# A threshold shift in rows of three in and rows of two out, half of each pair of batch 1 turned on TensorE, and no early projection of batch 0

## The chip, the cores and the metric

One core of one Trainium2 chip runs the whole program. The metric is device time in microseconds (us) of that core; below 2% counts as "same". Engines as the profile names them: PE (TensorE matmuls), PEld (its weight loads), DVE (VectorE), ACT (ScalarE), POOL (GpSimd), SP (SyncE, which issues most DMAs).

## The reference

```python
scores = q @ k.T / sqrt(64)                          # 8 batches, 8 heads, 576 x 64 each
thresh = max(scores, axis=-1) - tau                  # tau = 0.02
attn   = softmax(where(scores >= thresh, scores, -1e9))
x      = (attn @ v) as rows of 4608 x 512
h      = x @ w_in                                    # 512 x 2048
out    = (h - tanh(h)) @ w_out                       # 2048 x 512
```

## The kernel before

Two heads form a pair, four pairs a batch. A pair has nine tiles of 128 query rows: one mixed tile (rest rows of both heads) and four duos (two tiles, A and B). Tile by tile, in one static order: PE makes the scores, DVE evicts them and takes the row maximum, DVE turns the maximum into `tau - max` (the shift), ACT applies a very steep Prelu (the kink), the result is transposed on PE or by DMA, ACT takes exp, PE multiplies by V. The feed-forward layers of batch m run between the tiles of batch m+1: 16 hidden steps and 16 quarter projections, each four 128x512 matmuls. POOL prepares q, k and v.

The parts that the change touches:

```python
def on_pe(i):                          # which tiles are transposed on PE
    p, j = divmod(i, TPP)              # p: pair, j: tile of the pair
    return p < 6                       # all of batch 0, pairs 4 and 5 of batch 1
...
mx = const.tile([P, 3], F32)           # maxima of a duo; the third column stays 0
...
def shift(i):                          # once per duo, once per mixed tile
    n = 3 if kd == "B" else 1
    nc.vector.tensor_scalar(out=nb[:, 0:n], in0=mx[:, 0:n],
                            scalar1=-1.0, scalar2=tau, op0=ALU.mult, op1=ALU.add)
...
def split(p, t):                       # POOL, meanwhile, for each of q and k
    nc.gpsimd.tensor_scalar(out=x, in0=x, scalar1=QKSC, ...)          # 0.67 us
    nc.gpsimd.tensor_copy(out=hl[:, :, 0, :], in_=x)                  # 0.66 us
    nc.gpsimd.tensor_tensor(out=hl[:, :, 1, :], in0=x, in1=..., op=ALU.subtract)  # 1.28 us
...
pl, tag = (ps_h, "h") if i % 2 and i < HPAIR * TPP else (ps_y, "y")  # PSUM for PE's transposes
...
EARLY = lambda m: 3 if m else 3        # quarter projections done inside their own batch
```

## Time and profile before

| | us |
|---|---|
| timed runs, median (lowest to highest) | 549.77 (549.69 to 550.95) |
| the profiled run | 543.29 (span of the core 541.5) |
| duo shifts (128), in the profile | 41.0, mean 0.320 each |

### The profile page before, as it was taken

What the parts mean: (1) busy time and instruction counts of PE and PEld (TensorE: products, weight loads), DVE (VectorE), ACT (ScalarE), POOL (GpSimd) and SP (SyncE); (2) the same over time, 40 slices, a digit from 0 to 9 for tenths busy, and PEclk for the clock granted to TensorE, in tenths of its full rate; (3) what the DMA queues carried; (4) which work ended last, traced back from release to release, by engine and by line L of the source; (5) the groups of instructions that cost most, each with busy time, mean ns of one, the idle gap of its engine ahead of it and who ended that gap; (6) DMA issues with size and microseconds to landing.
All of it is one profiled execution on the core that took longest, in us unless ns stands there. A gap on an engine that the chain in (4) does not pass through costs nothing.

```text
span 541.5 us, 12959 instructions
## 1 busy us (share of the span) xinstructions
PE 506.7 (94%) x4704; PEld 288.0 (53%) x4771; DVE 445.9 (82%) x1203; ACT 438.3 (81%) x628; POOL 291.1 (54%) x390
## 2 busy tenths in 40 slices
PE   5999898989999999999999999999999999999997
PEld 3666565555555555555555555555555455444444
DVE  4999988989988999889888998899888887554440
ACT  4999888999898989899888989898989989533330
POOL 7999996767555666666545654566665620000000
PEclk9999999999999999999999999999999999999999
DMA  7554657999898998889999899698969975301113
GB/s 207 174 183 146 205 179 141 184 186 170 196 186 151 185 188 189 161 179 184 185 185 183 182 187 197 154 181 185 188 165 182 197 148 105 101 20 40 39 41 78
DMA packets 204768, 85.76 MB, mean 158 GB/s; under 512 B 172320, under 2 KB 197152, under 8 KB 204704
## 3 DMA queue, kind: packets, MB, share of 16 engines
q1 hardware_dynamic: 204112, 84.51, 72.6%
q8 instruction: 37, 0.61, 0.5%
q10 hardware_dynamic: 592, 0.43, 0.3%
q14 instruction: 27, 0.22, 0.1%
HBM read 36.70 MB, written 9.44 MB: 85 GB/s over the span
## 4 chain that ended last, share of the span: by engine, by line
PE 62%; DVE 24%; issue 5%; ACT 5%; DMA 3%; SPq 0%; DVEq 0%; ACTq 0%; POOL 0%
PE psY L510 18%; PE psH L484 16%; PE psS L319 13%; DVE sc L329 12%; PE psO L429 4%; DVE g L503 4%; PE psS L309 3%; PE ps_k L233 2%; PE psHt L484 2%; ACT pT L392 2%; ACT z L363 2%; DVE yo L520 2%; DMA qT<-qhl 2%; DVE nb L343 2%; DVE kT L256 1%
## 5 line engine op out<-in xcount | busy, mean ns | idle before, releaser
L329 DVE TENSOR_SCALAR_CACHE_REDUCE sc<-psS 128x576 f32<-128x576 f32 x288 | 215.7, 751 | 17.7 <-PE psS L319 10.4
L363 ACT ACTIVATE z<-sc,nb 128x576 bf16<-128x576 f32 x256 | 194.0, 771 | 22.9 <-DVE nb L343 22.4
L262 POOL COPY kS<-kT 64x1152 f16<-64x1152 f16 x62 | 70.9, 1143 | 132.6 <-DVE nb L343 130.9
L510 PE MATMUL psY<-w_out_sb,g 128*128 128x512 bf16 (+1 forms) x551 | 137.4, 373 | 4.1 <-DVE yo L520 1.6
L400 ACT ACTIVATE pT<-zT 128x1152 f16<-128x1152 bf16 (+1 forms) x130 | 139.1, 1070 | 0.0
L484 PE MATMUL psH<-xT,w_in_sb 128*128 128x512 bf16 x455 | 119.2, 379 | 7.2 <-DVE g L503 3.9
L319 PE MATMUL psS<-kT,qT 128*128 128x512 f16 (+1 forms) x512 | 104.9, 286 | 8.5 <-DVE sc L329 6.5
L497 ACT ACTIVATE th<-psH 128x512 f32<-128x512 f32 x128 | 75.5, 590 | 38.3 <-PE psH L484 37.7
L319 PEld LDWEIGHTS <-qT 128*128 128x128 f16 x1024 | 72.8, 97 | 58.1 <-issue 11.6
L503 DVE SCALAR_TENSOR_TENSOR g<-th,psH 128x512 bf16<-128x512 f32 x128 | 87.3, 682 | 19.0 <-ACT th L497 18.8
L319 PE MATMUL psS<-kS,qT 128*128 128x512 f16 x496 | 101.4, 286 | 0.0
L510 PEld LDWEIGHTS <-g 128*128 128x128 bf16 x592 | 50.7, 98 | 58.2 <-issue 5.7
L484 PEld LDWEIGHTS <-w_in_sb 128*128 128x128 bf16 x576 | 49.2, 98 | 59.7 <-issue 6.0
L429 PEld LDWEIGHTS <-pT 128*128 128x128 f16 x1280 | 55.7, 98 | 25.3 <-issue 1.7
L429 PE MATMUL psO<-vb,pT 128*128 128x65 bf16 x1280 | 61.2, 193 | 0.3
L343 DVE TENSOR_SCALAR nb<-mx 128x3 f32<-128x3 f32 (+1 forms) x160 | 45.6, 285 | 2.3
L186 POOL TENSOR_TENSOR khl<-kraw,khl 128x576 f16<-128x576 f32 x31 | 39.7, 1281 | 2.6
L186 POOL TENSOR_TENSOR qhl<-qraw,qhl 128x576 f16<-128x576 f32 x31 | 39.7, 1280 | 2.6
L392 ACT ACTIVATE pT<-psZ 128x640 f16<-128x640 bf16 (+1 forms) x54 | 35.4, 658 | 5.2 <-PE psZ L383 4.8
L256 DVE COPY kT<-ps_k 128x1152 f16<-128x1152 f16 x31 | 23.4, 756 | 13.3 <-PE ps_k L233 13.3
L520 DVE COPY yo<-psY 128x512 f32<-128x512 f32 (+1 forms) x33 | 22.5, 681 | 12.2 <-PE psY L510 7.6
L444 DVE TENSOR_TENSOR osb<-psO,rc 128x256 bf16<-128x256 f32 x64 | 27.2, 425 | 2.2
(78 smaller groups left out, 504.6 us busy)
## 6 DMA issues: line engine op xcount, KB each, us to landing
vraw<-in_v_dram SPq DMA_DIRECT2D x32, 256.0 KB, 3.5
out_dram<-yo SPq DMA_DIRECT2D x32, 256.0 KB, 2.8
kraw<-in_k_dram SPq DMA_DIRECT2D x31, 256.0 KB, 3.1
qraw<-in_q_dram SPq DMA_DIRECT2D x31, 256.0 KB, 3.9
wt<-in_moe_w_in_dram SPq DMA_DIRECT2D x8, 512.0 KB, 4.8
wt<-in_moe_w_out_dram SPq DMA_DIRECT2D x8, 512.0 KB, 3.9
zT<-z SPq DMA_TRANSPOSE x104, 3.5
kraw<-in_k_dram SPq DMA_DIRECT2D x32, 32.0 KB, 3.1
```

Of the source, the lines that this page charges most:

```text
L186: nc.gpsimd.tensor_tensor(out=hl[:, :, 1, :], in0=x, in1=hl[:, :, 0, :], op=ALU.subtract)
L262: nc.gpsimd.tensor_copy(out=o, in_=i)
L319: nc.tensor.matmul(out=ps[:, dst], lhsT=lhs, rhs=kk[:, src], start=(n == 0), stop=(n == 1),)
L329: nc.vector.tensor_scalar(out=sc, in0=ps[:, lo : lo + S], scalar1=SC, scalar2=None, op0=ALU.mult, op1=ALU.max, accum_out=mx[:, c : c + 1],)
L343: nc.vector.tensor_scalar(out=nb[:, 0:n], in0=mx[:, 0:n], scalar1=-1.0, scalar2=tau, op0=ALU.mult, op1=ALU.add,)
L363: nc.scalar.activation(out=z, in_=sc, func=ACT.Prelu, bias=nb, scale=1.0, alpha=STEEP)
L400: nc.scalar.activation(out=pt[:, 0 : n * P], in_=zts.pop(i)[:, 0:n, :], func=ACT.Exp)
L429: nc.tensor.matmul(out=po[:, (j - 1 - 5 * hh) + ab, :], lhsT=pt[:, blk * P : (blk + 1) * P], rhs=vb[:, hh, c, :], start=(n == 0), stop=(n ...
L484: nc.tensor.matmul(out=ps, lhsT=w_in_sb[:, c, n * P : (n + 1) * P], rhs=xs[m][:, c, :] if m < B else xR[:, c, :, :], start=(c == 0), stop= ...
L497: nc.scalar.activation(out=th, in_=ps, func=ACT.Tanh)
L503: nc.vector.scalar_tensor_tensor(out=gs[m][:, n, :], in0=th, scalar=-1.0, in1=ps, op0=ALU.mult, op1=ALU.add,)
L510: nc.tensor.matmul(out=ps, lhsT=gs[m][:, n, ms * P : (ms + 1) * P], rhs=w_out_sb[:, n, cols], start=(n == 0), stop=(n == DF_C - 1),)
```

## The change

The shift of a duo gets another access pattern. It must still deliver two numbers, but it now reads two rows of three (pitch 4) and writes three rows of two (pitch 3); elements 0 and 1 are the ones wanted. Batch 1 has two duos and the mixed tile of every pair transposed on PE, instead of the whole of pairs 4 and 5. This needs the last part: the projection of batch 0 no longer starts early, because its sum would hold the single `ps_y` buffer that those transposes use. (Half of each pair on PE with the early projection kept cannot be run: the build ends in a deadlock in the simulator.)

```diff
-        return p < 6
+        return p < HPAIR or p < 2 * HPAIR and j in (0, 1, 4, 5, 6)
-        mx = const.tile([P, 3], F32, name=f"mx{i}")
+        mx = const.tile([P, 8], F32, name=f"mx{i}")
-        n = 3 if kd == "B" else 1
-        nb = st_pool.tile([P, 3], F32, name="nb", tag="nb")
+        nb = st_pool.tile([P, 9], F32, name="nb", tag="nb")
+        o, m = nb[:, 0:1], mx[:, 0:1]
+        if kd == "B":
+            o = nb.rearrange("p (a b) -> p a b", b=3)[:, :, 0:2]
+            m = mx.rearrange("p (a b) -> p a b", b=4)[:, :, 0:3]
         nc.vector.tensor_scalar(
-            out=nb[:, 0:n], in0=mx[:, 0:n], scalar1=-1.0, scalar2=tau, ...
+            out=o, in0=m, scalar1=-1.0, scalar2=tau, ...
-        nbs[i] = nb[:, n // 2 : n // 2 + 1]
+            nbs[i - 1], nbs[i] = nb[:, 0:1], nb[:, 1:2]      # duo; mixed tile: nb[:, 0:1]
-    EARLY = lambda m: 3 if m else 3
+    EARLY = lambda m: 3 if m else 0
```

More of the change, by code (lines that the diff above doesn't have):

```diff
@@ L339, in shift @@
             return
-        n = 3 if kd == "B" else 1
         mx = mxs.pop(i)
-        nb = st_pool.tile([P, 3], F32, name="nb", tag="nb")
+        nb = st_pool.tile([P, 9], F32, name="nb", tag="nb")
[3 more added lines that the diff above has]
+            m = mx.rearrange("p (a b) -> p a b", b=4)[:, :, 0:3]
         nc.vector.tensor_scalar(
-            out=nb[:, 0:n], in0=mx[:, 0:n], scalar1=-1.0, scalar2=tau,
-            op0=ALU.mult, op1=ALU.add,
+            out=o, in0=m, scalar1=-1.0, scalar2=tau, op0=ALU.mult, op1=ALU.add
         )
-        nbs[i] = nb[:, n // 2 : n // 2 + 1]
         if kd == "B":
-            nbs[i - 1] = nb[:, 0:1]
+            nbs[i - 1], nbs[i] = nb[:, 0:1], nb[:, 1:2]
+        else:
+            nbs[i] = nb[:, 0:1]
     def kink(i):
```

## The prediction

> **What bounds the kernel now.** I read the page first (engine shares, chain that ended last), then the groups of DVE by shape, the chain in order of time, busy time by stretch, and the timeline around single shifts.
>
> ```profile
> PE 506.7 (94%) x4704; PEld 288.0 (53%) x4771; DVE 445.9 (82%) x1203; ACT 438.3 (81%) x628; POOL 291.1 (54%) x390
> PE 62%; DVE 24%; issue 5%; ACT 5%; DMA 3%; SPq 0%; DVEq 0%; ACTq 0%; POOL 0%
> ```
>
> PE is the bound on average, yet 24% of the chain that ended last lies on DVE, so in places PE waits for DVE. By stretch (columns: length, busy us and count of PE, PEld, DVE, ACT, POOL, granted clock, DMA share, GB/s):
>
> ```profile
> 30.00:60.00 30.00, 27.27 (x379) 19.10 (x378) 29.10 (x83) 29.07 (x48) 28.39 (x37) 1.00 0.61 190
> 60.00:90.00 30.00, 27.29 (x318) 18.20 (x320) 25.71 (x73) 25.79 (x43) 24.61 (x30) 1.00 0.49 147
> 90.00:120.00 30.00, 26.37 (x266) 15.40 (x268) 28.04 (x77) 28.23 (x40) 20.80 (x26) 1.00 0.99 185
> 240.00:270.00 30.00, 29.10 (x271) 16.20 (x276) 27.63 (x78) 27.44 (x38) 19.21 (x24) 1.00 0.93 185
> ```
>
> Three regimes. In batch 0 (about 14 to 60 us: no layer work yet) DVE and ACT are full and PE has slack. In batch 1 (60 to 125 us) nothing is full all the time; the chain changes between ACT, DVE and PE. From 125 to about 465 us PE is full, and the trace repeats every batch: batches 3 to 5 each last 58.8 us, with 2.1 us of PE idle in each. After 465 us only layer work is left, and the change does not touch it.
>
> The threshold shift is line 343. DVE's groups by shape:
>
> ```profile
> L343 DVE TENSOR_SCALAR nb<-mx 128x3 f32<-128x3 f32 x128 | 41.0, 320 | 2.3
> L343 DVE TENSOR_SCALAR nb<-mx 128x1 f32<-128x1 f32 x32 | 4.6, 144 | 0.0
> ```
>
> Three elements cost 320 ns on average and one costs 144; two elements cannot take 176 ns. Taken one by one, 79 of the 128 duo shifts take 166 ns on average, and 49 take over 200 ns, 27.9 us together. The timeline (start us, us, engine, line) shows what the long ones do:
>
> ```profile
> 209.21 1.28 POOL L186 TENSOR_TENSOR khl<-kraw,khl 128x576 f16<-128x576 f32 x1
> 209.28 1.24 DVE L343 TENSOR_SCALAR nb<-mx 128x3 f32<-128x3 f32 x1
> ...
> 48.21 1.28 POOL L186 TENSOR_TENSOR qhl<-qraw,qhl 128x576 f16<-128x576 f32 x1
> 48.67 0.14 DVE L343 TENSOR_SCALAR nb<-mx 128x1 f32<-128x1 f32 x1
> ```
>
> The shift of a duo starts 0.07 us after a POOL instruction and ends 0.03 us after that one's end (210.52 against 210.49). The one-element shift runs in the middle of the same POOL instruction in 0.14 us. All six of the 32 one-element shifts that overlap POOL work take 136 to 154 ns.
>
> **What the Trainium skill says.** "VectorE: DVE Perf Modes", section "Mode 2×_2P — use both read ports for one tensor": a one-source operation from SBUF to SBUF runs with both ports if the outermost non-unit dimension is even, "or odd and equal for src and dst". Three in and three out is the second case; one element has no such dimension. "SBUF — State Buffer", section "Who interferes with whom": the second port pair is shared with GpSimd, whoever issues first has it for the whole instruction and the other fully blocks; a DVE instruction with at most one SBUF input outside these modes does not contend. The trace agrees with both (1.24 us behind POOL, against 0.14 us). The new form reads two rows of three and writes three rows of two: the outer counts are 2 and 3, not both even and not equal, and the gaps (pitch 4 and pitch 3) keep the rows from being merged. By that rule it runs with one port. No trace here shows that form yet. The front page, "Trainium Kernel Development and Optimization", section "Performance Expectations", warns that matmul busy time is a bad metric because matmuls are pipelined; this trace agrees (four 128x512 matmuls show 1.03 us in the timeline and move the chain by 0.86), so I size PE work by the chain's 0.86.
>
> **The change part by part.**
>
> *Shift.* Six elements on one port: I estimate 150 ns, from 144 ns for one element and about 1 ns for each more. 128 x (320 - 150) = 21.8 us less DVE busy. How much of it counts depends on the regime.
>
> Batch 0: the shifts in the four pairs lose 1.1 to 1.4 us each over 170 ns, 4.9 us in all, and DVE is full. But ACT, which follows, is nearly full too: a pair takes about 11.6 us, and ACT's own issue spacing in its full stretches (nine kinks at 0.67, four duos of weights at about 0.5 + 0.6, one at 0.6) makes about 11.0. So about 0.4 to 0.5 of each 1.2 us is won: **-1.7 us**.
>
> From batch 2 on, one batch has 2.4 us of such excess, but the chain is mostly on PE. The chain in order of time (start us, us, what) where it leaves PE:
>
> ```profile
> 267.00 0.86 PE psH L484 x4
> 267.86 0.51 PE psS L319 x4
> ...
> 268.39 0.77 DVE sc L329 x2
> 269.15 0.60 DVE g L503
> ...
> 271.01 0.44 DVE nb L343
> 271.45 0.55 issue
> 271.99 0.75 DVE sc L329 x2
> ...
> 273.99 1.02 PE psH L484 x4
> ```
>
> That shift takes 1.07 us (0.90 over the usual); the gap of PE that ends the detour, 273.29 to 273.99, is 0.70. Hence all of it should go. A second gap of 0.42 us each batch (before psH at 302.57, waiting for xT, behind a shift of 0.68 us at 300.83) should go as well. The other gaps, about 0.9 us, wait for score evictions with no long shift ahead of them and stay. So 1.1 us a batch for batches 2 to 6, and about 0.4 in batch 7, where POOL runs out of work at 435 us: **-5.9 us**.
>
> *Half of each pair of batch 1 on TensorE.* Before, pairs 4 and 5 were turned on PE in full: 2 x (4 x 9 + 5) = 82 transposes, with 8 duos. Now pairs 4 to 7 each have two duos and the mixed tile: 4 x (2 x 9 + 5) = 92. PE gets 10 x 0.057 = +0.6 us, and ACT about the same (a duo costs it about 1.1 us in two pieces from PSUM, against 1.05 in one from SBUF). What changes is the spread: by the chain's pieces, pairs 4 and 5 needed about 14.5 us of PE each and took 15.6, while pairs 6 and 7 needed about 12.2 and were held by DVE.
>
> *No early projection for batch 0.* Three quarter projections, 3 x 0.86 = 2.6 us of PE work, go from batch 1 to batch 2 (the single PSUM buffer that holds the sum over them is now wanted by the transposes until the end of batch 1). With both parts each pair of batch 1 needs about 12.8 us of PE, 13.0 of DVE, 12.9 of ACT; with everything level I expect 13.8 in practice, against 57.6 / 4 = 14.4 now: **-2.8 us** with a little at its entry. Batch 2 is full of PE work, so the 2.6 us come back in whole: **+2.6 us**.
>
> Sum: -1.7 - 5.9 - 2.8 + 2.6 = -7.8 us. 549.8 - 7.8 = **542.0 us**.
>
> **The rivals.** (1) The new form still takes both ports, or its two-row patterns cost more than the wait they save. For it: no such form in this trace; against it: the one-element shift. Then the shift gives nothing, and only the other two parts remain: about 549.5. (2) DVE's time is mostly off the path: PE is 94% busy, and after one wait goes the next (score evictions through two PSUM buffers) takes its place, so only half of the 7.6 us arrives: about 546. (3) The waits feed each other: each shift holds the kink on ACT too (ACT waited 22.4 us for shifts in 28 places), and PE has 34 us of idle time, some 20 outside start and tail. If most of the 7.7 us of idle in batches 1 and 2 and the ACT waits went too, 537 to 538. (4) Batch 1 gets worse: transposes in all its pairs go through one PSUM buffer in lockstep with ACT. Against: they did so in pairs 4 and 5 already. It would cost some 3 us: 545. DMA at 0.99 in 90 to 150 us is no rival: no engine waits for a transposed tile there.
>
> **Range and chances.** Rivals 2 and 4 together give 546 as the upper end, rival 3 less a part 538.5 as the lower. Faster by over 2% needs 538.8 or less, 11 us of some 20 us of reachable idle time: 0.13. Slower by over 2% has nothing to carry it: 0.01.
>
> **What would show it.** Right: duo shifts about 150 ns with a maximum under 200, DVE busy near 424 us; the period of batches 3 to 5 down from 58.8 to about 57.7 with the gap before psH gone; batch 1 shorter by about 3 us, batch 2 longer than batch 3 by about 2.6. Wrong: shifts that still last to the end of a POOL instruction; a period that stays at 58.8 though the shifts are short; batch 2 not longer than batch 3.

## The result, and the profile after

The changed kernel takes 540.07 us (539.41 to 541.32) against 549.78 (549.69 to 550.95): ratio 0.9819, 95% interval 0.9804 to 0.9835. Ratios here are the mean time of one kernel's fast runs over that of the other's of the same rounds, so not quite the ratio of the medians quoted. Verdict: same at 2%, but 9.7 us faster and clear of noise.

The page after, shares of the engines and of the chain that ended last:

```profile
PE 509.5 (95%) x4781; PEld 287.1 (53%) x4781; DVE 428.8 (80%) x1203; ACT 437.0 (81%) x628; POOL 290.0 (54%) x390
PE 72%; DVE 12%; ACT 5%; POOL 4%; DMA 3%; issue 2%; SPq 0%; DVEq 0%; POOLq 0%; ACTq 0%
```

DVE's part of the chain is halved. All shifts together (duration ns min/median/max), first and last start, then the duo group alone:

```profile
L347 DVE TENSOR_SCALAR nb<-mx x160: 142/153/161, 10.5 to 455.9; 128x6 f32<-128x6 f32 x128, 128x1 f32<-128x1 f32 x32
L347 DVE TENSOR_SCALAR nb<-mx 128x6 f32<-128x6 f32 x128 | 19.9, 155 | 2.4
```

No shift waits any more: the maximum fell from 1240 to 161 ns, and the duo shifts from 41.0 to 19.9 us. The prediction showed one long shift behind POOL; in the whole profile before, all 49 shifts over 200 ns start while a POOL instruction runs, and 48 of them end within 0.05 us after it. The chain in order of time at the place that the prediction showed, one batch period in:

```profile
268.31 0.86 PE psH L488 x4
269.17 0.49 PE psS L320 x4
269.66 0.88 PE psY L514 x4
270.54 0.02 issue
270.56 0.69 DVE yo L524
271.25 0.61 DVE g L507
271.86 0.04 issue
271.90 1.02 PE psH L488 x4
```

The detour over DVE took 5.6 us before (268.39 to 273.99); it takes 1.3 now, and PE's gap there fell from 0.70 to 0.32 us. What is left is an eviction (`yo`) and a gating (`g`) in a row; no shift is in it.

One reading to beware of: the page before showed POOL idle for 130.9 us ahead of `kS`, put down to the shift. It is 128.8 after. POOL waits there for the copy of `kT`; a shift had merely sent the semaphore event that came last. That figure never was a cost.

Busy time by stretch after, in the columns of the prediction:

```profile
30.00:60.00 30.00, 27.56 (x384) 18.88 (x380) 26.55 (x83) 29.16 (x49) 28.40 (x36) 1.00 0.61 192
60.00:90.00 30.00, 25.66 (x295) 16.48 (x295) 26.11 (x77) 26.34 (x40) 26.60 (x34) 1.00 0.80 193
90.00:120.00 30.00, 25.92 (x297) 16.19 (x294) 26.51 (x78) 28.62 (x45) 21.42 (x28) 1.00 0.65 135
240.00:270.00 30.00, 30.00 (x280) 16.56 (x279) 26.76 (x78) 27.77 (x40) 19.52 (x26) 1.00 0.98 186
```

In batch 0 DVE falls from 29.10 to 26.55 of 30 us, but ACT stays full at 29.2. In the periodic part PE reaches 30.00 in the stretch shown. In batch 1 (60 to 120 us) PE is busy less than before, and idle more.

Yet the two profiled spans differ by only 3.7 us (541.5 and 537.8), where the timed runs differ by 9.7. The first experiment is about that.

### The profile page after: what moved, and what is told of

It is laid out like the page before. It is cut to its first block, busy times and chain, and to the rows that moved or that the text cites. A ratio compares the mean times of both kernels' runs of the same rounds, so it can differ in the third digit from the quotient of the medians.

```text
span 537.8 us, 13031 instructions
## 1 busy us (share of the span) xinstructions
PE 509.5 (95%) x4781; PEld 287.1 (53%) x4781; DVE 428.8 (80%) x1203; ACT 437.0 (81%) x628; POOL 290.0 (54%) x390
## 4 chain that ended last, share of the span: by engine, by line
PE 72%; DVE 12%; ACT 5%; POOL 4%; DMA 3%; issue 2%; SPq 0%; DVEq 0%; POOLq 0%; ACTq 0%
PE psY L514 21%; PE psH L488 18%; PE psS L320 16%; DVE sc L330 5%; PE psO L433 5%; PE psS L310 3%; PE ps_k L234 3%; DVE g L507 2%; ACT z L367 2%; PE psHt L488 2%; ACT pT L396 2%; DMA qT<-qhl 2%; DVE yo L524 2%; POOL kS L263 1%; DVE kT L257 1%
## 5 line engine op out<-in xcount | busy, mean ns | idle before, releaser
L514 PE MATMUL psY<-w_out_sb,g 128*128 128x512 bf16 (+1 forms) x592 | 145.8, 374 | 1.6 <-DVE yo L524 1.6
L263 POOL COPY kS<-kT 64x1152 f16<-64x1152 f16 x62 | 70.7, 1141 | 130.5 <-DVE nb L347 128.8
L404 ACT ACTIVATE pT<-zT 128x1152 f16<-128x1152 bf16 (+1 forms) x128 | 137.4, 1074 | 0.0
L488 PE MATMUL psH<-xT,w_in_sb 128*128 128x512 bf16 x480 | 124.0, 379 | 2.4 <-DVE g L507 2.4
L396 ACT ACTIVATE pT<-psZ 128x640 f16<-128x640 bf16 (+1 forms) x56 | 36.9, 661 | 4.0 <-PE psZ L387 3.7
L234 PE MATMUL ps_k<-ident_f,khl 128*128 128x128 f16 x288 | 21.7, 220 | 5.7 <-DVE khl L200 5.6
```

The costliest lines, as they stand in the source:

```text
L263: nc.gpsimd.tensor_copy(out=o, in_=i)
L396: nc.scalar.activation(out=pt[:, off * P : (off + n) * P], in_=ps[:, 0 : n * P], func=ACT.Exp)
L404: nc.scalar.activation(out=pt[:, 0 : n * P], in_=zts.pop(i)[:, 0:n, :], func=ACT.Exp)
L488: nc.tensor.matmul(out=ps, lhsT=w_in_sb[:, c, n * P : (n + 1) * P], rhs=xs[m][:, c, :] if m < B else xR[:, c, :, :], start=(c == 0), stop= ...
L514: nc.tensor.matmul(out=ps, lhsT=gs[m][:, n, ms * P : (ms + 1) * P], rhs=w_out_sb[:, n, cols], start=(n == 0), stop=(n == DF_C - 1),)
```

## The experiments

Stretches below run from the copy that ends one batch's attention (`xR`) to that of the next, so each is one batch.

**e1: the kernel before again, unchanged.** 

> The kernel before, unchanged. Its timed runs lay at 549.7 to 551.0 us, but its profiled execution at 543.3, while the changed kernel's profiled and timed executions agree (539.6 and 540.1). Theory A: the kernel before has two ways of running, because how long its shifts wait for POOL depends on how the two engines happen to fall together; then a new profile may show 541 or some 548 us of span, and the longer one has more time in the shifts (over 30 us for the 49 or more long ones). Theory B (rival): something about the profiled run or its chip alone was faster; then the new profile has the same shift times (about 41 us for the duo shifts) whatever its span. Timed against itself: ratio 1.00 within 0.3%.

Measured: 549.93 us (549.72 to 551.27), ratio 1.0003; the runs of the kernel before on the same chip lay between 545.47 and 551.01. The profiled run took 551.27, span 549.5, and its duo shifts cost 48.9 us, not 41.0; its 66 shifts over 200 ns take 38.7 us, where the early profile's 49 take 27.9:

```profile
L343 DVE TENSOR_SCALAR nb<-mx 128x3 f32<-128x3 f32 x128 | 48.9, 382 | 2.2
```

Theory A holds. Busy time over one period (columns as before), first the early profile, then this one, then the changed kernel:

```profile
243.60:302.43 58.83, 56.77 (x533) 31.89 (x542) 53.46 (x147) 52.47 (x73) 34.57 (x45) 1.00 0.90 181
```

```profile
247.44:307.56 60.12, 57.33 (x542) 31.88 (x542) 55.04 (x147) 52.72 (x73) 34.51 (x44) 1.00 0.92 176
```

```profile
241.89:299.85 57.96, 57.28 (x543) 31.90 (x542) 51.28 (x147) 52.32 (x73) 34.44 (x45) 1.00 0.96 183
```

(The early profile lacks nine matmul records per period, 533 against 542, so its PE time is about half a microsecond too small.) The kernel before has two periods, 58.8 and 60.1 us, and in each of these two profiles keeps to one for batch after batch. The timeline shows what decides. First the early profile, near the end of a period:

```profile
239.90 0.17 DVE L343 TENSOR_SCALAR nb<-mx 128x3 f32<-128x3 f32 x1
239.92 0.41 PE L319 MATMUL psS<-kT,qT 128*128 128x512 f16 x2
...
240.00 1.28 POOL L186 TENSOR_TENSOR khl<-kraw,khl 128x576 f16<-128x576 f32 x1
```

Then the same shift and the same POOL instruction in e1:

```profile
242.48 1.28 POOL L186 TENSOR_TENSOR khl<-kraw,khl 128x576 f16<-128x576 f32 x1
242.53 1.32 SPq L371 DMA_TRANSPOSE zT<-z  x1
242.55 1.23 DVE L343 TENSOR_SCALAR nb<-mx 128x3 f32<-128x3 f32 x1
...
244.50 0.41 PE L319 MATMUL psS<-kT,qT 128*128 128x512 f16 x2 [1.28 <-DVE sc L329]
```

In the first, the shift starts 0.10 us ahead of POOL and takes 0.17. In the second it starts 0.07 us behind and takes 1.23, the score eviction comes late, and PE stands for 1.28 us. That is the difference of the two periods, and it comes back every batch: three of a period's four pairs take the same time in both profiles (14.9, 15.7 and 15.1 us), the fourth 13.15 and 14.48. Of the 8.0 us between the two spans, 6.6 lie in batches 2 to 6. In later sets the runs of the kernel before lay between 543.49 and 551.25 us, down to a median of 545.12 on one chip. I take the values between as executions that keep the short period for some batches and the long one for others; no profile caught one doing so.

**e2, e3, e4: the parts of the change alone**, on the chip of e1. The edits against the kernel before:

```diff
 e2_shift_only: the new shift;      p < 6 and EARLY(0) = 3 kept
 e3_half_only:  half-turned pairs and EARLY(0) = 0;   old shift kept
 e4_early_only: EARLY(0) = 0;       p < 6 and the old shift kept
```

> Only the new form of the shift, pairs 4 and 5 turned on TensorE in full and the early projection of batch 0 kept. Theory A (the prediction): the shift carries the gain, 7.6 us of it: about 542 us, ratio 0.986, and if the whole gain is the shift's, 540 us and 0.982. Rival: the gain needs the levelled batch 1; then it stays above 546 us (ratio over 0.993). In the profile: duo shifts about 155 ns, none over 200, period of batches 3 to 5 about 58.0 us.

> Only half of each pair of batch 1 on TensorE with no early projection of batch 0; the old form of the shift. Theory A: -2.8 in batch 1 and +2.6 in batch 2, so 549.5 us, ratio 0.998 to 1.002. Rival: it is worth 2 us or more by itself, 547.5 or less (ratio under 0.996).

> Only the early projection of batch 0 taken away (three quarter projections, 2.6 us of PE work, go from batch 1 to batch 2); pairs 4 and 5 in full on TensorE, old shift. Theory A: batch 2 is full of PE work and pays 2.6 us, batch 1 is not and gives back 1 to 1.5: about 551 us, ratio 1.002 to 1.004. Rival: batch 1 gives back all of it: ratio 1.000.

| | time, us | ratio to before | 95% interval | batch 1 | batch 2 | batches 3 to 6, each |
|---|---|---|---|---|---|---|
| e1, before | 549.93 | 1.0003 | 0.9983 to 1.0024 | 57.6 | 60.2 | 60.1 |
| e2, shift | 539.21 | 0.9801 | 0.9782 to 0.9819 | 56.4 | 58.5 | 58.0 |
| e3, half-turned, no early | 551.27 | 1.0026 | 1.0003 to 1.0050 | 58.1 | 62.0 | 60.1 |
| e4, no early | 549.09 | 0.9983 | 0.9962 to 1.0003 | 55.0 | 61.7 | 60.1 |
| changed kernel | 540.07 | 0.9819 | 0.9804 to 0.9835 | 56.8 | 60.2 | 58.0 |

The shift alone gives all of the gain and a little more. The other parts do nothing or cost: e3 is 2.2 us slower than e4, so under the old shift half-turning costs, and its loss lies in batch 1 (58.1 against 55.0). My expectation for e4 was too high, its rival right: batch 1 gave back all of the 2.6 us and batch 2 paid only 1.6.

**e5: is it the two ports?** The changed kernel with two rows of three written instead of three rows of two.

```diff
-            o = nb.rearrange("p (a b) -> p a b", b=3)[:, :, 0:2]
+            o = nb[:, 0:8].rearrange("p (a b) -> p a b", b=4)[:, :, 0:3]
```

> The changed kernel with one thing altered: the shift of a duo writes two rows of three, as it reads them, instead of three rows of two. Same six elements, same gaps. Theory A (two ports): both outer counts are now 2, so the shift takes both ports and waits for POOL again: duo shifts with a maximum over 1.0 us and a mean over 300 ns, time back at 549 to 552 us (the kernel with the old shift and the same other parts took 551.3). Rival (the gain comes from the number or the layout of the elements, or from the pitch): shifts stay near 155 ns, time stays at 540.

Measured: 551.13 us (550.15 to 551.46), ratio 1.002 (0.9997 to 1.0043); duo shifts 49.2 us, mean 384 ns; period 60.1 us. All shifts:

```profile
L347 DVE TENSOR_SCALAR nb<-mx x160: 135/170/1268, 11.0 to 467.7; 128x6 f32<-128x6 f32 x128, 128x1 f32<-128x1 f32 x32
```

The profile prints both forms as 128x6, six elements in and six out. One has outer counts 2 and 2 and waits up to 1268 ns; the other has 2 and 3 and never exceeds 161 in the profile after. The whole gain is gone. So the way in which the output is laid out in rows decides, not the number of elements. The edit changes the length and pitch of the output's rows together with their count, and no run tells these apart: that it is the count is the rule that the prediction started from. Nor was the form run without gaps between the rows, so the need for gaps is not shown.

**e6: is the row form needed?** The changed kernel with two shifts of one element each.

```diff
-        nc.vector.tensor_scalar(out=o, in0=m, ...)
+        for c in range(2 if kd == "B" else 1):
+            nc.vector.tensor_scalar(out=nb[:, c : c + 1], in0=mx[:, c : c + 1], ...)
```

> The changed kernel with the shift of a duo as two instructions of one element each. Theory A: one element takes one port, so neither waits for POOL (maximum under 200 ns, mean about 144 ns), and the price is 128 more instructions of 70 to 145 ns, 9 to 18 us of DVE time, where DVE is not the bound mostly hidden: 541 to 544 us, clearly under the 551.3 us of the old shift with the same other parts. Rival (the gain needs the row form): 548 or more.

Measured: 540.20 us (539.23 to 541.17), ratio 0.9823 (0.9794 to 0.9851):

```profile
L344 DVE TENSOR_SCALAR nb<-mx x288: 141/148/156, 10.2 to 456.8; 128x1 f32<-128x1 f32 x144
```

(The view takes its shapes from every second instruction, hence x144.) No shift waits, and the 128 instructions more cost nothing that can be measured. DVE's busy time rises by 5.0 us (433.8 against 428.8), not by the 9 to 18 expected. So the gain does not need the row form: both forms that do not wait for POOL give it. What cost time was the wait, not the work.

**e7 to e10: what half-turning costs**, all on one further chip, five rounds. e7 is the changed kernel again. The others against it:

```diff
 e8_after_pair9_on_pe
-        return p >= 2 * HPAIR and (p % 2 == 1 or p == 30)        # q transposed by DMA
+        return p >= 10 and (p % 2 == 1 or p == 30)
 e9_shift_early
-        return p < HPAIR or p < 2 * HPAIR and j in (0, 1, 4, 5, 6)
+        return p < 6
 e10_shift_early_pair9: both edits
```

> The changed kernel, unchanged, to stand on one chip beside the next three: 540.1 us, ratio 0.982. Theory A (no second way of running without the shared port): period of batches 3 to 5 at 57.97 us again, spread of all runs under 2 us.

> The changed kernel, but the queries of pair 9 are turned on TensorE instead of by DMA. In the changed kernel PE waits 2.1 us at 117.8 us for that DMA, which took 5.1 us to land behind the transposes of the tiles. Theory A: that wait is what the half-turned batch 1 lost; without it 2.1 less 0.5 us for nine more transposes on PE: about 538.5 us, ratio 0.979. Rival: another wait takes its place, 540 us.

> New shift and no early projection of batch 0, but pairs 4 and 5 in full on TensorE: the changed kernel without the half-turned pairs. Theory A (half-turning costs about 1.5 us beyond what it levels): 538.5 us, ratio 0.9795, below the changed kernel and about at the shift alone (539.2). Rival (the prediction's): half-turning gains 2.8 us together with the early part, so this one is slower than the changed kernel: 541 or more.

> As the run before, with the queries of pair 9 turned on TensorE too. Here the wait for that DMA was short (0.2 to 0.3 us with the shift alone), so by theory A it gains nothing and PE pays 0.5 us: 538.5 to 539.5 us. Rival: it gains as much as in the run with half-turned pairs, 537 us.

| | time, us | ratio to before | batch 1 | batch 2 |
|---|---|---|---|---|
| e7 changed kernel | 540.30 (539.41 to 541.41) | 0.9879 | 56.7 | 60.1 |
| e8 pair 9 on PE | 539.86 (539.51 to 541.13) | 0.9872 | 56.7 | 60.1 |
| e9 shift and no early | 538.96 (538.40 to 539.47) | 0.9854 | 53.9 | 60.7 |
| e10 e9 with pair 9 on PE | 539.22 (538.62 to 540.36) | 0.9858 | 55.0 | 60.1 |

(The ratios are nearer to 1 because the kernel before ran at 548.06 us here, from 544.85 to 549.67.) e7 repeats to 0.2 us, with a period of 57.95, so the changed kernel shows no second way of running in its two profiles. Its spread of 2.0 us is just the bound I had set. e9 shows that half-turning itself costs 1.3 us: 2.8 in batch 1, partly given back later. e8 tested one suspect. The changed kernel's timeline, line of the wait:

```profile
119.92 0.42 PE L320 MATMUL psS<-kT,qT 128*128 128x512 f16 x2 [2.11 <-DMA qT<-qhl]
```

Without that DMA the wait is gone, but in e8 two others, absent in e7, stand near it:

```profile
117.55 0.41 PE L320 MATMUL psS<-kT,qT 128*128 128x512 f16 x2 [0.68 <-DVE sc L330]
...
122.06 0.41 PE L320 MATMUL psS<-kT,qT 128*128 128x512 f16 x2 [0.69 <-DVE sc L330]
```

Together with the added PE work of about 0.5 us they about make up for it: taking this DMA away wins nothing. My theory for e8 was wrong, its rival right. e10, as expected, gains nothing.

**e11, e12: is it the single PSUM buffer?** Transposes of batch 1 by turns in `ps_y` and `ps_h`; e11 on the changed kernel, e12 on e9.

```diff
-            pl, tag = (ps_h, "h") if i % 2 and i < HPAIR * TPP else (ps_y, "y")
+            pl, tag = (ps_h, "h") if i % 2 and i < 2 * HPAIR * TPP else (ps_y, "y")
```

> The changed kernel, but in batch 1 the tiles turned on TensorE go by turns into the one PSUM buffer they have now and into those of the hidden layer, as they do in batch 0. Theory A (prediction's rival 4: the single buffer ties PE and ACT together in all four pairs, and that is where the half-turned pairs lose their 2.4 us in batch 1): batch 1 shorter by 1 to 2 us, the gap of 1.15 us before psZ at 68 us gone, about 538.8 us. Rival (the loss lies in the pairs' score evictions and in pair 9's queries, not in this buffer; or the hidden layer then lacks its buffers): 540 us or more.

> The same buffers with pairs 4 and 5 in full on TensorE and the new shift, the fastest form so far (538.96). Theory A: the waits of pairs 4 and 5 for that buffer shrink, 538 us. Rival: the hidden layer's two buffers are the scarcer ones, 539 us or more.

Measured: e11 540.42 us (540.37 to 541.26), e12 539.36 (538.43 to 539.83); batch 1 takes 57.2 and 54.5 us, both longer than without. The gap of 1.15 us before `psZ` at 68 us is gone. But before `psH`, whose two buffers the transposes now share, stand four gaps of about 0.4 us (1.69 in all) where the changed kernel has two (0.83), and two gaps of 0.65 us before `psZ` now wait for DVE's gating of the hidden layer. The theory falls, the rival stands. The ratios of 0.992 and 0.989 come from the kernel before, whose median was 545.12 us on this chip.

The best form measured is e9, 538.96 us; the shift alone (539.21) cannot be told from it.

## Why the prediction was right or wrong

The time (542.0, range 538.5 to 546.0, measured 540.07) and the verdict were right. The mechanism of the shift, a wait for POOL that depends on the form of the instruction, was right and is shown by e2, e5 and e6. (That two ports stand behind it is the account that the prediction cites; the runs show the wait.) The sum behind the number was not right: two errors cancelled, and that 540.07 fell near 542.0 is partly luck.

| term | predicted | measured, profile to profile | against e1's profile |
|---|---|---|---|
| batch 0 | -1.7 | -1.4 | -2.6 |
| batch 1 | -2.8 | -0.8 | -0.8 |
| batch 2 | +2.6 - 1.1 | +1.3 | 0.0 |
| batches 3 to 6 | -4.4 | -3.4 | -8.6 |
| batch 7 and tail | -0.4 | +0.6 | +0.3 |
| sum | -7.8 | -3.7 | -11.7 |

- **Baseline.** The step that failed first was "549.8 - 7.8": I worked out savings from a profile whose run took 543.3 us and took them from runs of 549.8. The missing 6.5 us were contention too, in another phase, and the change removed them as well. Batches 3 to 6 therefore gave about 2.15 us each (60.1 to 58.0) against the usual runs, where I had counted 1.1. e1's profiled run, at 551.27, was itself at the upper edge, so its column overshoots the measured 9.7.
- **Shift, periodic part.** Against its own profile, 0.85 us per batch instead of 1.1. The "second gap of 0.42 us" went in whole; the first shrank from 0.70 to 0.32 only, since `yo` and `g` follow each other on DVE whatever the shift does.
- **Shift, batch 0.** "ACT, which follows, is nearly full too" held: DVE lost 2.55 us of busy time in 30, ACT stayed at 29.2, and batch 0 became 1.4 us shorter. But it is not shown that these 1.4 us are the shift's. From the first `xR` copy to the fourth, the shift alone (e2) takes 38.8 us, as the kernel before does, and the changed kernel 38.1; the first copy itself falls anywhere from 28.9 to 30.9 us in the 14 profiles (29.3 to 30.9 with the old shift or e5's, 28.9 to 30.3 with those that do not wait). In all, e2's batch 0 ended 0.4 us earlier than in the early profile (68.4 to 68.0), so the -1.7 counted too much.
- **Shift, work.** A duo shift takes 155 ns, where I had said 150. DVE's busy time fell by 17.1 us (445.9 to 428.8), not by 21.8: the shifts lost 21.1 us, but part of that time overlaps other DVE instructions in the profile.
- **Batch 1.** "With everything level I expect 13.8 in practice" failed. A pair took 14.2. From e1 to e2, e2 to e9 and e9 to e7 the parts are: shift 1.2 us won; no early projection 2.5 won; half-turning 2.8 lost. Level demand on three engines did not give level progress. Why the half-turned pairs lose is not settled: pair 9's DMA (e8) and the single buffer (e11) are each not enough to explain it. PE's gaps over 0.15 us between 60 and 126 us sum to 8.3 us in the changed kernel and 5.4 in e9: 1.2 more before pair 9's queries, 1.1 more before transposes, most of the rest before score matmuls that wait for DVE's evictions. No one of them is shown to be the cause.
- **Batch 2.** It is 2.2 us longer than batch 3 (60.15 against 57.97), where I had said 2.6.
- **Rivals.** 1 (still two ports) is refuted by the trace after. 2 (only half of the shift's 7.6 us arrives) was partly right, profile to profile: the shift alone shortened the span by 5.0 us (541.5 to 536.5), and 1.2 of these lie in batch 1, where I had no term for the shift alone. 3 (waits feed each other) comes nearest: a shift that starts 0.07 us late delays DVE, then PE, and keeps the same unlucky order in the next batch. It was no case of hidden idle time, as I had argued, but of a profile in the lucky phase. 4 (batch 1 worse) came true in its result but not by its buffer.

What puts an execution into one period or the other, and when it changes, stays open.

## What to carry to other kernels

If a profiled run and the timed runs of the same kernel differ by more than the change is expected to give, settle that first; the profile may show a phase that is rare. Look for tiny instructions with a wide spread: a mean of 320 ns at a median near 169 and a maximum of 1240 is a wait written down as work, and it can be removed by a form that does not need the contended resource, even one with more elements or more instructions. A part of a change that should level a stage must be run alone; here it cost 1.3 us and hid behind the gain of the other.

## What the Trainium skill lacked or had wrong

- "VectorE: DVE Perf Modes", section "Mode 2×_2P — use both read ports for one tensor": its rule on outer counts held in every form tried (2 and 2: up to 1268 ns in e5; 2 and 3: at most 163 in the eight profiles with that form). The section does not say that the mode brings nothing at this size, though the fixed cost per instruction that the page gives further down hints at it: undelayed shifts of three elements on two ports took 166 ns on average, six elements on one port 155, and one element 144 to 148.
- "SBUF — State Buffer", section "Who interferes with whom": it says that issue order decides who blocks, and the traces agree for the DVE side (0.17 us ahead, 1.23 us behind); no delay of GpSimd behind a shift is shown here. It gives ratios for a blocked instruction, but not how soon it ends after the other (here 0.03 us), and does not say that a periodic kernel can settle into the lucky or the unlucky order, with periods of 58.8 or 60.1 us and runs of the same kernel from 543.5 to 551.3 us.
- Neither of these pages tells how to recognise such a port wait in a profile: it is counted as the instruction's own duration, not as idle time before it, so the chain names the shift (2% and 4% of the span in the two profiles of the kernel before) and never GpSimd.
